# First-stage bursts one step earlier and spread relayout loads in a Fourier mixing and MLP kernel

## The chip, the cores and the metric

The kernel runs on one core of a Trainium2 chip. The metric is the device time of one execution in microseconds. A core has five engines that run on their own and wait for each other through semaphores: TensorE (PE, matmuls; PEld is its weight load), VectorE (DVE), ScalarE (ACT), GpSimd (POOL) and SyncE (SP). In this kernel POOL and SP mostly issue DMA transfers, each from its own queue in order.

## The reference, cut to what matters

```python
X = np.fft.rfft(x, axis=1)                       # x: 8 batches x 3008 rows x 256 channels
Y = X * (filt_r + 1j * filt_i)[None]             # 1505 frequencies x 256 channels
y = np.fft.irfft(Y, n=3008, axis=1)
h = y.reshape(24064, 256) @ w_in                 # 256 -> 2048
s = np.sin(alpha * h)
out = (h + s * s / (alpha + 1e-9)) @ w_out       # 2048 -> 256
```

So each batch goes through a long Fourier transform, a product with a filter and the transform back, and then all 24064 rows go through two matrix products with a sine between them.

## The kernel before

**The second half is the backbone.** The rows are cut into 48 chunks, for pairs of batches, of 512 rows (the one in twelve that starts at column 2560 has 384). `hidden(k, jb)` makes one of 16 blocks of the hidden layer of chunk k: two matmuls `ph` (line 602), a cosine on ACT into `cos_all` (L606), and one operation on DVE that makes `v` (L607). `project(k, u)` multiplies eight blocks of `v` with `w_out` into `po` (L622); ACT copies the sums to `o` (L631), and POOL issues their stores (L666).

**The planner.** The main loop goes through steps. One step has two calls of `hidden` for chunk k, then `slot(step)`, then the projections of chunk k−1 that fall to this step (eight matmuls `po` for each), then `slot(step + 0.5)`. Everything of the Fourier transforms is put into a list beforehand, each entry with the step at which it is due (`put`), and `slot` takes out what is due, in order of due time, with at most one entry of PE work per slot unless an entry is more than a step late. The order of instructions on every engine comes from this list alone. A chunk is eight steps, a pair of batches 96, and the plan of batch b is laid out around z = 48 b, the step at which its rows are first needed.

**The stages of a batch b ≥ 2.**

- `load_x` (L160, POOL): part ch of four of the input, two transfers, due 8 steps ahead of its burst. Each also waits for the last `v` that was issued before it (`after(ins, marks["snake"])`).
- `first_tiled` (L222), a *first-stage burst*: eight matmuls `pa` on a quarter of the array each. They fill four PSUM buffers: two of the pool `fps` (two buffers in all, which `forward` and `last` use too, and `inverse_tiled`) and two of the pool `hps` (four buffers, otherwise used by `ph`). ACT evacuates two of them (L185) and DVE two (L187), and SP stores the result to the scratch tensor `d1` in DRAM (L229).
- `load_t2` (L235, POOL), the *relayout loads*: four loads g of 384 KB from `d1`, in another order of the axes.
- `forward` (L243, 12 units): two matmuls `pb`, evacuated by ACT to `xf` (L246); SP swaps the halves into `xs` (L250). `product` (L257) and `cross` (L263, L264) on DVE multiply with the filter. Loads g = 0 to 3 feed units 0 to 2, 3 to 5, 6 to 8 and 9 to 11.
- `inverse_tiled` (L293), an *inverse burst*, three per batch: sixteen matmuls `pc` into two buffers of `fps` and two of `hps`, three evacuations on ACT and one on DVE, and stores to `d2` (L301).
- `load_t4` (L306, SP) and `last` (L316, 16 blocks u): four matmuls `pd` into one buffer of `fps`, evacuated into `y`, two on ACT to one on DVE in turn (L185, L187).

Batch 1 uses smaller forms of the first stage (L206) and of the inverse (L274), and batch 0 is done ahead of the loop. A buffer of a pool is free again when the evacuation of its last user is done; the next matmul into it waits for that on PE, and with it all that stands behind it.

**Due times that matter here.** `firsts(b)` gives the steps of the four bursts of a batch. For b ≥ 4 they are 48 b − 105.5 + 8 ch. `inverses(b)` gives those of the inverse bursts. `bursts` collects them all. `aside` moves a `product` or a `cross` that is due in the 1.1 steps ahead of a burst to just behind it, and `clear` moves a `forward` or a `last` that would fall right at a burst:

```python
    bursts = [at for b in range(TILED, B) for at in (*firsts(b), *inverses(b))]
...
        return next((s + 1 for s in bursts if s - 0.75 < at <= s + 0.25), at)
...
        return next((s + 0.05 for s in bursts if s - 1.1 < at <= s), at)
```

A `product` follows its `forward` by 1.5 steps and a `cross` by 4.5. Block u of `last` is due at z − 6.5 + u for u < 4 and at z − 11 + 2.6 u after that; block 6 thus at z + 4.6, which `slot(z + 5)` takes, and block 9 at z + 12.4. The forward units of batches 1 and 2 are due from step 18 in steps of 1.21 and from step 51 in steps of 2.2. The bursts of batch 3 are due at 49.5, 54.5, 60.5 and 66.5.

Of the kernel before, what the change touches and what calls it, by code (L numbers as in the profile page):

```python
# [71 lines left out]
def kernel(  # L72
# [599 lines left out]
    def put(at, fn, *args, pe=False):  # L672
        pending.append((at, len(pending), pe, fn, args))

    def firsts(b):

        return {2: (37.5, 39.5, 41.5, 43.5), 3: (49.5, 54.5, 60.5, 66.5)}.get(
            b, [48 * b - 105.5 + 8 * ch for ch in range(4)])

    def inverses(b):  # L680

        return (63.5, 73.5, 81.5) if b == 2 else [48 * b - 46.5 + 16 * w for w in range(3)]

    bursts = [at for b in range(TILED, B) for at in (*firsts(b), *inverses(b))]

    def clear(at):

        return next((s + 1 for s in bursts if s - 0.75 < at <= s + 0.25), at)

    def aside(at):  # L690

        return next((s + 0.05 for s in bursts if s - 1.1 < at <= s), at)
# [9 lines left out]
    for b in range(1, B):  # L702
        s = s1 if b == 1 else Spectral(b)
        z = 48 * b
        if b > 1:
            for ch in range(4):
                put(22 + 4 * ch if b == 2 else firsts(b)[ch] - 8, s.load_x, ch)
        if b < TILED:
            for i in range(16):
                put(6.9 + 0.35 * i, s.first, i, pe=True)  # L710
        else:
            for ch in range(4):
                put(firsts(b)[ch], s.first_tiled, ch, pe=True)
        for g in range(4):
            put(12.5 if b == 1 else 45 if b == 2 else max(70, z - 77 + 12 * g), s.load_t2, g)
        for u in range(12):
            inv = 24 + 1.21 * u if b == 1 else 57 + 2.2 * u if b == 2 else z - 59 + 4 * u
            fwd = inv - 6
            fwd = clear(fwd)
            put(fwd, s.forward, u, pe=True)  # L720
            put(aside(fwd + (0.5 if b == 1 else 1.5)), s.product, u)
            if s.fused:
                put(aside(fwd + (4 if b == 1 else 4.5)), s.cross, u)
            if b < TILED:
                put(inv, s.inverse, u, pe=True)
        if b >= TILED:
            for w in range(3):
                put(inverses(b)[w], s.inverse_tiled, w, pe=True)
        for ch in range(4):
            put(z - (9.5 if b == 1 and ch < 3 else (10.5, 10.5, 10.5, 3)[ch]), s.load_t4, ch)  # L730
        for u in range(16):
            put(clear(z + (u - (5 if b == 1 else 6.5) if u < 4 else 2 * u - 9 if b == 1 else 2.6 * u - 11)),
                s.last, u, pe=True)
# [59 lines left out]
```

## Time and profile before

| | |
|---|---|
| Median of 3 runs | 776.32 us (775.06 to 776.39) |
| The profiled execution's own time | 775.76 us |
| Its span, first to last instruction | 774.0 us |
| Busy: PE, DVE, ACT, POOL | 763.1, 656.5, 611.4, 371.1 us |
| Granted TensorE clock | 1.0 of full speed, all through |
| `ph` L602, `po` L622 on PE | 389.1 us (1536 matmuls), 389.3 us (3008) |
| `v` L607 on DVE, `cos_all` L606 on ACT | 482.8 us, 414.0 us (768 each) |
| Burst matmuls `pa` L222 | 192, from 111.8 to 528.3 us |
| Relayout loads L235 | 28, 384 KB each, median 5.1 us from issue to landing |

How to read it. Busy time of PE is the time in which a matmul is under way, with ends that are modelled, so back-to-back matmuls overlap in the record; starts of matmuls tell more than ends. A line of the timeline gives the start and the length of a run of like instructions on one engine, in microseconds, then engine, line, operation, output and input, and their number; in brackets stands the idle time of the engine before it and who ended it. The list of waits gives engine, line and releaser, then the total in microseconds, the number of waits and the longest.

### The profile page before, as it was taken

The numbers are of one execution on the slowest core, as the hardware profiler recorded it, in microseconds if no ns is written. First come the engines' busy times: TensorE is split into PE (matmuls) and PEld (weight loads), VectorE is DVE, ScalarE is ACT, GpSimd is POOL, SyncE is SP. The second block draws the span as 40 slices with busy tenths as digits, with TensorE's granted clock in tenths as the row PEclk, the third lists the DMA queues.
The fourth block names the chain that finished last, engine by engine and source line by source line (L and its number), as shares of the span: only waits on it lengthen the run. The fifth ranks groups of instructions, "written<-read, shape, count | busy, mean of one in ns | idle before, by whom it ended". The sixth has DMA issues, their size and how long they took to land.

```text
span 774.0 us, 17223 instructions
## 1 busy us (share of the span) xinstructions
PE 763.1 (99%) x6036; PEld 516.6 (67%) x6036; DVE 656.5 (85%) x1172; ACT 611.4 (79%) x1206; POOL 371.1 (48%) x649
## 2 busy tenths in 40 slices
PE   8999999999999999999999999999999999999997
PEld 4757766666666667666666666766666666766666
DVE  6886998999989888898889988899888888777774
ACT  6798988898888877888878787888778777777763
POOL 6455446544645555555565647554554645330000
PEclk9999999999999999999999999999999999999999
DMA  9955678854855438544474536764254322511112
GB/s 221 285 107 168 139 157 262 206 136 111 218 140 138 118 71 221 139 115 124 113 201 109 141 92 151 199 148 120 72 145 106 92 69 55 138 47 32 40 37 60
DMA packets 81518, 101.49 MB, mean 131 GB/s; under 512 B 18884, under 2 KB 60864, under 8 KB 81431
## 3 DMA queue, kind: packets, MB, share of 16 engines
q1 hardware_dynamic: 53503, 52.84, 25.7%
q0 software_dynamic: 27440, 47.29, 25.6%
q8 instruction: 47, 0.77, 0.4%
q14 instruction: 40, 0.33, 0.1%
q10 hardware_dynamic: 488, 0.27, 0.1%
HBM read 56.15 MB, written 46.66 MB: 133 GB/s over the span
## 4 chain that ended last, share of the span: by engine, by line
PE 90%; DMA 4%; DVE 3%; ACT 1%; issue 0%; POOL 0%; SPq 0%; POOLq 0%
PE po L622 41%; PE ph L602 40%; DVE v L607 3%; PE pd L316 2%; PE pb L243 2%; PE pa L222 2%; DMA d_t<-d_tbl 1%; PE pc L293 1%; DMA w_out<-in_moe_w_out_dram 1%; DMA filt_t<-in_filt_r_dram 1%; DMA w_in<-in_moe_w_in_dram 1%; ACT cos_all L606 1%; PE pa L206 0%; PE pc L274 0%; POOL x L168 0%
## 5 line engine op out<-in xcount | busy, mean ns | idle before, releaser
L607 DVE SCALAR_TENSOR_TENSOR v<-cos_all,ph 128x512 f16<-128x512 f32 (+1 forms) x768 | 482.8, 672 | 95.6 <-ACT cos_all L606 92.3
L606 ACT ACTIVATE cos_all<-ph 128x512 f32<-128x512 f32 (+1 forms) x768 | 414.0, 600 | 99.5 <-PE ph L602 98.2
L666 POOL DMA_DIRECT2D out_dram<-o x530 | 291.7, 557 | 242.4 <-ACT o L631 214.9
L602 PE MATMUL ph<-y,w 128*128 128x512 f16 (+1 forms) x1536 | 389.1, 375 | 1.3 <-DVE v L607 1.1
L622 PE MATMUL po<-w,v 128*128 128x256 f16 x3008 | 389.3, 273 | 0.0
L622 PEld LDWEIGHTS <-v 128*128 128x128 f16 x3008 | 290.1, 98 | 84.2 <-issue 1.1
L602 PEld LDWEIGHTS <-w 128*128 128x128 f16 x1536 | 143.2, 98 | 113.9 <-issue 19.0
L631 ACT COPY o<-po 128x512 f32<-128x512 f32 (+1 forms) x95 | 56.1, 590 | 7.8 <-PE po L622 7.2
L246 ACT CAST xf<-pb 128x512 f16<-128x512 f32 x84 | 51.1, 608 | 1.3 <-PE pb L243 0.8
L185 ACT CAST y<-pd 128x376 f16<-128x376 f32 (+1 forms) x86 | 42.1, 491 | 12.3 <-PE pd L316 8.8
L160 POOL DMA_DIRECT2D x<-in_x_dram x48 | 25.6, 538 | 41.7 <-DVE v L607 26.9
L185 ACT CAST t_h<-pa 128x512 f16<-128x512 f32 (+1 forms) x60 | 32.8, 590 | 12.5 <-PE pa L222 11.3
L316 PEld LDWEIGHTS <-t_a 96*128 96x128 f16 x448 | 31.4, 97 | 12.7
L264 DVE TENSOR_TENSOR p<-p,xs 128x512 f16<-128x512 f16 x84 | 35.7, 425 | 2.9
L263 DVE TENSOR_TENSOR xs<-xs,filt_t 128x512 f16<-128x512 f16 x84 | 35.2, 419 | 2.0 <-DMA xs<-xf 2.0
L257 DVE TENSOR_TENSOR p<-xf,filt_t 128x512 f16<-128x512 f16 x84 | 35.1, 419 | 0.0
L185 ACT CAST gt<-pc 128x512 f16<-128x512 f32 x54 | 28.2, 595 | 8.4 <-PE pc L293 8.4
L187 DVE CAST t_h<-pa 128x512 f16<-128x512 f32 (+1 forms) x52 | 33.5, 683 | 0.2
L243 PE MATMUL pb<-t,d_t 128*128 128x256 f16 x168 | 32.1, 273 | 0.0
L316 PE MATMUL pd<-wh_t,t_a 96*128 96x94 f16 x384 | 31.8, 204 | 0.0
L235 POOL DMA_DIRECT2D t<-d x28 | 24.4, 874 | 11.3 <-DMA d<-t_h 9.4
L243 PEld LDWEIGHTS <-d_t 128*128 128x128 f16 x168 | 16.3, 98 | 14.3
(70 smaller groups left out, 276.4 us busy)
## 6 DMA issues: line engine op xcount, KB each, us to landing
t<-d POOLq DMA_DIRECT2D x28, 384.0 KB, 5.1
xs<-xf SPq DMA_DIRECT2D x168, 64.0 KB
t_a<-d SPq DMA_DIRECT2D x28, 384.0 KB
x<-in_x_dram POOLq DMA_DIRECT2D x50, 188.0 KB, 4.5
d<-t_h SPq DMA_DIRECT2D x48, 192.0 KB
d<-gt SPq DMA_DIRECT2D x36, 256.0 KB
out_dram<-o POOLq DMA_DIRECT2D x91, 64.0 KB, 2.1
out_dram<-o POOLq DMA_DIRECT2D x31, 80.0 KB, 3.5
```

Source lines behind the costliest of these rows:

```text
L185: marks["act"] = nc.scalar.copy(out=dst, in_=src)
L243: nc.tensor.matmul(out=ps[:, i, :], lhsT=d_t[:, s, :], rhs=self.t2[s // 6][:, s % 6, :], start=True, stop=True)
L246: nc.scalar.copy(out=self.xf[u], in_=ps)
L263: nc.vector.tensor_tensor(out=xs, in0=xs, in1=f_t[1][:, 2 * u:2 * u + 2, :], op=ALU.mult)
L264: nc.vector.tensor_tensor(out=p, in0=p, in1=xs, op=ALU.add)
L316: nc.tensor.matmul(out=psv[:, i, :], rhs=wi_t if self.b < TILED else wh_t, start=True, stop=True, lhsT=t4_h[ch // 2][0:NK, n0 % 16 + i, cb ...
L602: nc.tensor.matmul(out=ps[:, 0:n], lhsT=w1[:, cb, jb * 128:jb * 128 + 128], rhs=y_cols[:, cb, c0:c0 + n], start=(cb == 0), stop=(cb == 1))
L606: nc.scalar.activation(out=cs[:, 0:n], in_=ps[:, 0:n], func=AFT.Sin, bias=float(np.pi / 2))
L607: marks["snake"] = nc.vector.scalar_tensor_tensor(out=v[k][:, jb, 0:n], in0=cs[:, 0:n], scalar=-1.0, in1=ps[:, 0:n], op0=ALU.add, op1=ALU. ...
L622: nc.tensor.matmul(out=pso[k][:, t % 2, :], lhsT=v[k][:, jb, 128 * t:128 * t + 128], rhs=w2[:, jb, :], start=(jb == 0), stop=(jb == 15))
L631: copy(out=o[:, i0:t % 2 + 1, :], in_=pso[k][:, i0:t % 2 + 1, :])
L666: queues[i % len(queues)].dma_start(out=bass.AP(tensor=out.tensor, offset=out.offset + t0 * C, ap=[*ap, [1, C]]), in_=o_blk[p0:p0 + rows, :])
```

## The change

All four first-stage bursts of each batch from 4 on come one step sooner, which moves their `load_x` one step sooner with them, and `bursts` as well. The second load of batch 3 (ch = 1) is due at step 45 instead of 46.5. The four relayout loads of batch 1 are due at steps 13.5, 14, 17 and 20 instead of all at 12.5, and those of batch 2 at 46.5, 49, 53 and 59 instead of all at 45.

```diff
     def firsts(b):
         return {2: (37.5, 39.5, 41.5, 43.5), 3: (49.5, 54.5, 60.5, 66.5)}.get(
-            b, [48 * b - 105.5 + 8 * ch for ch in range(4)])
+            b, [48 * b - 106.5 + 8 * ch for ch in range(4)])
...
             for ch in range(4):
-                put(22 + 4 * ch if b == 2 else firsts(b)[ch] - 8, s.load_x, ch)
+                put(22 + 4 * ch if b == 2 else 45 if (b, ch) == (3, 1) else firsts(b)[ch] - 8, s.load_x, ch)
...
         for g in range(4):
-            put(12.5 if b == 1 else 45 if b == 2 else max(70, z - 77 + 12 * g), s.load_t2, g)
+            put((13.5, 14, 17, 20)[g] if b == 1 else (46.5, 49, 53, 59)[g] if b == 2 else max(70, z - 77 + 12 * g), s.load_t2, g)
```

## The prediction, made before the result was known

> **What bounds the kernel now.** I read the page first, parts 1 and 4 (busy time, and the chain that ended last):
>
> ```profile
> PE 763.1 (99%) x6036; PEld 516.6 (67%) x6036; DVE 656.5 (85%) x1172; ACT 611.4 (79%) x1206; POOL 371.1 (48%) x649
> ...
> PE 90%; DMA 4%; DVE 3%; ACT 1%; issue 0%; POOL 0%; SPq 0%; POOLq 0%
> ```
>
> PE is busy for 99% of the span and carries 90% of the chain. Ends of matmuls are modelled, so I next asked for PE's own waits between 66 and 764 us, the stretch in which everything that the change touches lies:
>
> ```profile
> PE ph L602 <- DVE v L607: 0.6, 3, 0.2
> PE pd L403 <- ACT xf L246: 0.4, 1, 0.4
> ```
>
> The reader sees total, times and longest: 1.0 us in 698. Busy time can hide waits under the modelled ends, so I went through the starts of PE's matmuls in the timeline. Two hidden blocks and 8 projections, one step of the planner, take 1.74 us. A first-stage burst adds 0.65 us, all 24 the same to within 3 ns, so none of the 16 that move waits now. Three inverse bursts (L293) do wait: 0.41 us near 181 us, 0.53 us near 319 and 0.53 us near 503. PE is the bound, and only what makes it wait, or stop waiting, counts.
>
> **The bursts (16, each one step sooner).** The built programs have the same 6036 matmuls, 1172 DVE and 1206 ACT operations; SP's order is the same. Each burst (8 matmuls) passes 4 matmuls `ph` and 8 `po`; its two ACT and two DVE evacuations pass two `cos_all` and two `v`; and one product L257 (0.42 us on DVE) goes from two steps ahead of the burst to just behind it, since `aside` now catches it. So PE's work stays the same: 0 us. What decides is whether the PSUM buffers are free one step sooner. The pair of the four-buffer pool waits for the same distance in `v` as now: 0. The pair of the two-buffer pool `fps` takes the buffers of the two last users. For parts 0, 1 and 3 of a batch the last user lies at least a whole step back. For part 2 it doesn't: block 6 of the last stage (planned at z+4.6, run at step z+5) stood 1.5 steps ahead of the burst, and now stands half a step ahead. Batch 6, timeline:
>
> ```profile
> 419.41 1.04 PE L622 MATMUL po<-w,v 128*128 128x256 f16 x8
> ...
> 420.29 1.03 PE L602 MATMUL ph<-y,w 128*128 128x512 f16 x4
> ...
> 421.00 0.55 DVE L187 CAST y<-pd 128x376 f16<-128x376 f32 x1
> ...
> 422.12 0.63 PE L222 MATMUL pa<-x,wt_t 47*64 47x512 f16 x8
> ```
>
> Columns: start, length, what; block 6's matmuls `pd` stand just ahead, at 419.24. The burst will stand where `ph` starts at 420.29. A burst starts 0.09 us later than a `ph` there (last `po` of eight starts at 421.92; a `ph` would follow 0.11 later, the burst starts at 422.12), so at 420.38. The `y` evacuation, queued on DVE behind two `v`, ends at 421.55 only, or about 421.4 with the product gone from ahead of it. Here the built program puts both `fps` tiles of the burst in one bank, the second waiting for ACT's cast of the first. The cast starts 0.45 us behind a burst (row below: 314.00, 314.45), takes 0.59, and PE starts 0.05 after (a `v` ends at 320.06, `ph` starts at 320.11): 0.45 + 0.59 + 0.05 = **1.09 us**.
>
> In batches 4, 5 and 7 the second tile waits for ACT's `y`. Batch 5:
>
> ```profile
> 326.69 0.51 ACT L185 CAST y<-pd 128x376 f16<-128x376 f32 x1
> ...
> 326.91 0.59 PE L602 MATMUL ph<-y,w 128*128 128x512 f16 x2
> ```
>
> The burst would start at 326.91 + 0.09 = 327.00; its second tile may start at 327.20 + 0.05 = 327.25: 0.25 us. Batch 7, likewise: `ph` at 510.71, `y` 510.50 to 511.00: 0.25 us. Batch 4: `ph` at 236.48, `y` ends at 236.66: 0.14 us. Behind such a wait PE's whole queue stands; nothing later waits now, so nothing gives it back. Sum: 1.09 + 0.25 + 0.25 + 0.14 = +1.73 us.
>
> The waits near 319 and 503 come five to six us behind a moved burst. The first of them:
>
> ```profile
> 314.00 0.63 PE L222 MATMUL pa<-x,wt_t 47*64 47x512 f16 x8
> 314.45 1.07 ACT L185 CAST t_h<-pa 128x512 f16<-128x512 f32 x2 [0.67 <-PE pa L222]
> ...
> 316.62 0.65 ACT L631 COPY o<-po 128x512 f32<-128x512 f32 x1
> ...
> 317.46 2.15 ACT L606 ACTIVATE cos_all<-ph 128x512 f32<-128x512 f32 x4
> ...
> 320.11 1.19 PE L602 MATMUL ph<-y,w 128*128 128x512 f16 x4 [0.19 <-DVE v L607]
> ```
>
> ACT has no gap from 316.16 to 319.62: copies and casts push `cos_all` to 317.46, hence `v` to 318.18, hence PE. With the burst's casts one step sooner, ACT is free earlier, but its copy at 316.62 needs the last `po`, which ends at 316.47: it can start at 316.52, 0.10 us sooner. So 0.10 of 0.53 us goes, twice: −0.2 us; bounds 0 and −1.06. What is late next is that copy.
>
> The Trainium skill speaks against the move: "TensorEngine Tiling (Array Packing)", Performance Considerations, holds that tiling speeds up TensorE but not the PSUM evacuation, which may become the limit. By that rule alone every moved burst would wait for a cast as batch 6's does, 16 x 1.09 = 17 us. The trace agrees only in part: three of the inverse bursts wait, none of the first-stage bursts does, so by the rows the four cases above stay the sum.
>
> **The relayout loads.** Batch 1: loads 0 and 1 keep their place on POOL; 2 and 3 go behind 7 and 14 output stores. They have the room: they land at 73.6 and 74.9 us now and their first forward matmuls come at 87.3 and 94.7. Moved by about 4 and 10 us, both still land ahead. Cost 0. Batch 2 on POOL:
>
> ```profile
> 130.16 3.34 POOL L235 DMA_DIRECT2D t<-d  x4 [3.62 <-DMA d<-t_h]
> 133.49 1.10 POOL L160 DMA_DIRECT2D x<-in_x_dram  x2
> ```
>
> Load 0 waits for batch 2's `d` stores, lands at 133.97, and the forward matmul needs it at 137.26: 3.3 us of room. The change puts the two loads of `x` part (3,1) ahead of it, into POOL's idle time; they share the DMA engines with the last `d` store. Bounds: nothing, and 2.0 us (two such loads land 1.0 us apart) plus a landing of 5.0 us instead of 3.8: 3.2 us, within the room. I take 0. Loads 1 to 3 then stand behind stores that take 0.53 us each, with 13, 25 and 37 us of room. `x` (3,1) lands 1.5 us ahead of its burst now and some 10 after; that gain is 0 in this execution. The `x` loads of batches 4 and later keep their order on POOL and land 5.4 us or more ahead; a step costs 1.74 of that.
>
> **Sum.** +1.73 − 0.2 + 0 = +1.5 us. The profiled execution took 775.76 us (span 774.0), so 777.3; it lies 0.56 under the median of the runs, 776.32, so the median should be **777.8**.
>
> **Rivals.**
> 1. *No wait at part 2*: three of four waits are under 0.3 us, and if `y` comes out first and the one-bank case costs little, what is left is −0.2: 776.1. Against it: the bank order stands in the built program.
> 2. *Slower: load 0 of batch 2 becomes the wait.* If the `d` store and then the load each lose more than the room of 3.3 us together, PE stops at the first forward matmul of batch 2, priced 1 us for 4.3 us lost: 778.8. It decides from a landing at 137.26. For it: the DMA engines are 100% busy from 124 to 127 us. Against: they are all but idle from 130.1 to 131.6, and can catch up there.
>    The Trainium skill gives such a delay a cause, "SBUF — State Buffer", SBUF: two separate sides: while DVE holds the shared port, GpSimd can't write descriptors, and a transfer of 620 ns took 3100. By it, an estimate of 2.5 us on load 0, still within its room; the 28 issues of L235 take 825 to 904 ns each, so this trace shows no such lock.
> 3. *Faster*: both inverse waits vanish (−1.06), part 2 is free, and in usual executions `x` (3,1) comes late today (the median lies 0.56 above the profile): 776.32 − 1.06 − 0.56 = 774.7.
>
> **Chances.** A measurement can tell about 0.2% from no change: 1.55 us, 774.77 to 777.87. Forecast, 777.8, sits just under the edge: 0.62, split by the gain near 319 and 503, 0.37 within and 0.25 above. Rival 1: 0.16, within. Rival 2: 0.16, above. Rival 3: 0.06, below. So faster 0.06, same 0.53, slower 0.41. Range 775.6 to 779.0: the low end is rival 1 less the 0.56 us by which usual executions exceed the profile, should a late `x` (3,1) be what they lose; the high end is rival 2 with no gain near 319 and 503.
>
> **What would show it.** In the profile after: PE starting `pa` twice, 1.1 us apart, near 420 us, and shorter breaks near 237, 327 and 511; the break near 319 and 503 still some 0.4 us; load 0 of batch 2 landing ahead of its `pb`. Wrong if PE shows no break within a part 2 burst, or one at the first `pb` of batch 2.

## The result, and the profile after

The changed kernel took 776.87 us (median of 15 runs, 776.32 to 778.23), the kernel before 775.29 (median of 15 runs taken beside them, 774.85 to 776.79). The ratio is 1.0017, with a 95% interval of 1.001 to 1.0024: **1.6 us slower**, where +1.5 was forecast. The median of before is 1.0 us lower than that of the three runs from which the prediction started, so the time itself, 777.8, was forecast 0.9 too high; the difference was not.

The page after, parts 1 and 4:

```profile
PE 763.4 (99%) x6036; PEld 516.9 (67%) x6036; DVE 656.6 (85%) x1172; ACT 612.7 (79%) x1206; POOL 370.9 (48%) x649
...
PE 90%; DVE 4%; ACT 3%; DMA 2%; issue 1%; POOL 1%; POOLq 0%
```

PE has the same work and is as busy as before. ACT has 3% of the chain instead of 1%, but that isn't the loss: most of it lies in the first 66 us, ahead of everything that the change moves, where the chain passes through ACT for 13.3 us in this profile and for 2.0 in the one before. The list of PE's waits from 66 to 764 us names the place:

```profile
PE pa L222 <- ACT t_h L185: 0.7, 1, 0.7
PE pd L403 <- ACT xf L246: 0.4, 1, 0.4
PE ph L602 <- DVE v L607: 0.2, 1, 0.2
```

The first line wasn't there before: a burst matmul waits for ACT's cast of the same burst. It is the burst of batch 6, part 2, in the timeline:

```profile
419.21 0.33 PE L316 MATMUL pd<-wh_t,t_a 96*128 96x94 f16 x4
...
420.35 0.40 PE L222 MATMUL pa<-x,wt_t 47*64 47x512 f16 x2
420.80 0.58 ACT L185 CAST t_h<-pa 128x512 f16<-128x512 f32 x1 [0.73 <-PE pa L222]
420.81 0.54 DVE L187 CAST y<-pd 128x376 f16<-128x376 f32 x1
421.43 0.62 PE L222 MATMUL pa<-x,wt_t 47*64 47x512 f16 x6 [0.68 <-ACT t_h L185]
```

The eight `pa` are broken in two: two matmuls at 420.35, six at 421.43. Between them ACT's cast runs from 420.80 to 421.38. PE shows 0.68 us idle, but from start to start the break is 1.08 us: the first part ends, as modelled, only at 420.75. The other three breaks of part 2 don't show as idle time at all; I read them from the starts of the `pa`, where an undisturbed burst takes 761 ns from the start of the matmul ahead of it (a `po`) to the start of the one behind it (a `ph`):

| burst, part 2 of batch | at us | takes ns | break us | predicted |
|---|---|---|---|---|
| 4 | 236.22 | 886 | 0.13 | 0.14 |
| 5 | 326.61 | 1005 | 0.24 | 0.25 |
| 6 | 420.35 | 1836 | 1.08 | 1.09 |
| 7 | 511.68 | 1003 | 0.24 | 0.25 |

In batches 4, 5 and 7 the third `pa`, the first one into the second buffer of `fps`, starts 0.05 us behind the end of ACT's `y` of block 6. Batch 5:

```profile
326.30 0.51 ACT L185 CAST y<-pd 128x376 f16<-128x376 f32 x1
326.61 0.87 PE L222 MATMUL pa<-x,wt_t 47*64 47x512 f16 x8
```

That `y` ends at 326.80, the third `pa` starts at 326.85. Behind the burst of batch 5 there is one more break, not foreseen: the third `ph`, at 328.00, starts 0.15 us late. The inverse bursts near 319 and 503 us still wait, 0.36 us each instead of 0.53. Here is the first:

```profile
316.29 0.58 ACT L631 COPY o<-po 128x512 f32<-128x512 f32 x1
...
317.13 2.09 ACT L606 ACTIVATE cos_all<-ph 128x512 f32<-128x512 f32 x4
...
317.78 2.48 DVE L607 SCALAR_TENSOR_TENSOR v<-cos_all,ph 128x512 f16<-128x512 f32 x4 [0.51 <-ACT cos_all L606]
...
318.95 0.63 PE L293 MATMUL pc<-p,e_t 64*64 64x256 f16 x16
```

Measure each from the inverse burst: the copy starts 2.66 us ahead of it (2.56 before: 319.18 − 316.62), the first `v` 1.17 (1.00 before). The relayout loads of batch 2 and `x` (3,1), in the timeline of POOL:

```profile
127.19 1.05 POOL L160 DMA_DIRECT2D x<-in_x_dram  x2 [0.99 <-PE ph L602]
130.28 0.88 POOL L235 DMA_DIRECT2D t<-d  x1 [2.03 <-DMA d<-t_h]
```

Load 0 lands at 134.61, 2.3 us ahead of its `pb`; `x` (3,1) lands at 133.16, 8.8 us ahead of its burst.

For all that follows one number stands for each kernel, *the stretch*: the time from the start of the 289th `ph` matmul to that of the 1249th, about 177 to 637 us. It holds every burst of batches 4 to 7. PE's order outside the moved work is the same in it, so it repeats to within 0.02 us where the programs are alike. Before: 459.31 us. After: 460.78, so +1.47. The breaks above give 1.69 + 0.15 − 0.17 − 0.17 = +1.50. That accounts for the result.

### The profile page after: what moved, and what is told of

It reads as the page before. It is cut to its first block, busy times and chain, and to the rows that moved or that the text cites. A ratio compares the mean times of both kernels' runs of the same rounds, so it can differ in the third digit from the quotient of the medians.

```text
span 774.8 us, 17223 instructions
## 1 busy us (share of the span) xinstructions
PE 763.4 (99%) x6036; PEld 516.9 (67%) x6036; DVE 656.6 (85%) x1172; ACT 612.7 (79%) x1206; POOL 370.9 (48%) x649
## 4 chain that ended last, share of the span: by engine, by line
PE 90%; DVE 4%; ACT 3%; DMA 2%; issue 1%; POOL 1%; POOLq 0%
PE po L622 41%; PE ph L602 40%; DVE v L607 3%; PE pd L316 2%; PE pb L243 2%; PE pa L222 2%; DMA w<-id 1%; PE pc L293 1%; ACT t_h L185 1%; ACT cos_all L606 1%; PE pa L206 0%; ACT xf L494 0%; PE pd L403 0%; PE warm L437 0%; DMA x<-in_x_dram 0%
## 5 line engine op out<-in xcount | busy, mean ns | idle before, releaser
L264 DVE TENSOR_TENSOR p<-p,xs 128x512 f16<-128x512 f16 x84 | 35.7, 425 | 2.9
L263 DVE TENSOR_TENSOR xs<-xs,filt_t 128x512 f16<-128x512 f16 x84 | 35.0, 416 | 0.5 <-DMA xs<-xf 0.5
L257 DVE TENSOR_TENSOR p<-xf,filt_t 128x512 f16<-128x512 f16 x84 | 34.9, 417 | 0.0
L235 POOL DMA_DIRECT2D t<-d x28 | 24.7, 884 | 9.7 <-DMA d<-t_h 8.3
```

The costliest lines, as they stand in the source:

```text
L263: nc.vector.tensor_tensor(out=xs, in0=xs, in1=f_t[1][:, 2 * u:2 * u + 2, :], op=ALU.mult)
L264: nc.vector.tensor_tensor(out=p, in0=p, in1=xs, op=ALU.add)
```

## The experiments

My theory: PE waits in part 2 for the buffers of `fps`, because block 6 of `last` now stands half a step ahead of the burst; all else is worth little. The rivals were that the relayout loads cost the time, or that every moved burst costs a share. Each ratio is to the kernel before, run beside it, with its 95% interval.

**1. The bursts alone, and the loads alone.**

The kernel `bursts_only` is the changed one with

```diff
-                put(22 + 4 * ch if b == 2 else 45 if (b, ch) == (3, 1) else firsts(b)[ch] - 8, s.load_x, ch)
+                put(22 + 4 * ch if b == 2 else firsts(b)[ch] - 8, s.load_x, ch)
...
-            put((13.5, 14, 17, 20)[g] if b == 1 else (46.5, 49, 53, 59)[g] if b == 2 else max(70, z - 77 + 12 * g), s.load_t2, g)
+            put(12.5 if b == 1 else 45 if b == 2 else max(70, z - 77 + 12 * g), s.load_t2, g)
```

and `loads_only`, the same kernel as `loads_again`, is the changed one with

```diff
-            b, [48 * b - 106.5 + 8 * ch for ch in range(4)])
+            b, [48 * b - 105.5 + 8 * ch for ch in range(4)])
```

> The bursts of batches 4 and later one step sooner, loads as before. Theory (the short waits of PE within the part 2 bursts are the whole cost): the same breaks as after, +0.12, +0.24, +1.08 and +0.24 us in the part 2 bursts near 236, 327, 420 and 512 us, +0.15 at the ph behind the one near 327, -0.17 each at the inverse bursts near 319 and 503; in all some 1.5 us above before, as after. Rival (the loads cost the time): within 0.3 us of before.

> The loads moved as in the change, the bursts where they were. Theory: PE's breaks as in before, load 0 of batch 2 landing some 2 us ahead of its first pb; within 0.3 us of before. Rival (the loads cost the time): some 1.5 us above before, with a new break of PE between 60 and 150 us.

> The same kernel as in the run with the loads alone, measured once more, since that one came out at a ratio of 0.9991 with an interval that ends at 0.9999. Theory (the loads are worth nothing, PE's path between 177 and 637 us is that of before): within 0.3 us of before, the interval around 1. Rival (x part (3,1), which landed only 0.8 to 1.5 us ahead of its burst in three profiles with the old loads, lands late in some executions, and the change mends this): again 0.3 to 0.5 us below before.

The bursts alone: 776.96 us, ratio 1.0019 [1.001, 1.0029], stretch 460.78, as after, with the same breaks at the same bursts. The loads alone: 775.12, ratio 0.9991 [0.9982, 0.9999], stretch 459.30, as before. That interval just misses 1; the same kernel run again gave 775.74, 0.9997 [0.9983, 1.0011], stretch 459.30. The loads are worth nothing that can be told. `x` (3,1) landed 8.2 us ahead of its burst with them and 0.8 without (the kernel with the bursts alone): room that nothing used in any profile.

**2. Part 2 put back, and part 2 alone.**

The kernel `part2_back` is the changed one with

```diff
-            b, [48 * b - 106.5 + 8 * ch for ch in range(4)])
+            b, [48 * b - 106.5 + 8 * ch + (ch == 2) for ch in range(4)])
```

and `part2_alone` is the kernel before with

```diff
-            b, [48 * b - 105.5 + 8 * ch for ch in range(4)])
+            b, [48 * b - 105.5 + 8 * ch - (ch == 2) for ch in range(4)])
```

> The changed kernel with only the part 2 bursts of batches 4 to 7 back at their old step. Theory: the four breaks of part 2 and the one behind the burst near 327 us are gone, the gains near 319 and 503 us stay (they belong to other parts): 0.3 us below before and 1.8 below after. Rival (moving any burst costs, or the loads do): three quarters of the 1.5 us stay, 1.2 us above before, with breaks elsewhere.

> The kernel before with only the part 2 bursts of batches 4 to 7 one step sooner. Theory: the breaks of part 2 alone, 0.12 + 0.24 + 1.08 + 0.24 us, with 0.15 behind the second of them: 1.7 to 1.85 us above before, and the waits near 319 and 503 us unchanged at 0.53 each. Rival (each moved burst costs alike): a quarter of 1.5 us, 0.4 above before.

Part 2 alone: 777.3 us, ratio 1.0019 [1.0011, 1.0028], stretch 460.98, +1.67. Its four bursts take 886, 1004, 1836 and 1003 ns, and the inverse waits stay at 0.53. A quarter of the moved bursts thus holds all of the loss. But the 0.15 us expected behind the burst of batch 5 did not come. DVE's order is the same there as after the change; what differs is the wait near 319, still 0.53. Where that wait is 0.17 shorter, PE reaches the burst sooner and DVE doesn't: its first `v` behind the last `cross` starts 1.13 us ahead of the burst after the change, 1.30 with part 2 alone. So the 0.15 is the gain near 319 given back eight us later.

Part 2 put back: 775.72, 1.0 [0.9991, 1.0009], stretch 459.30. The four breaks are gone, as the theory had it. The 0.3 us below before did not come: the gains near 319 and 503 are there (0.17 each), but new breaks of 0.2 us behind part 2 of batch 5 (near 329) and 0.16 behind part 3 of batch 6 (near 437), now seven steps behind part 2, take them back.

**3. Which engine empties block 6.** Of the four blocks 6 that stand ahead of a part 2 burst, the one ahead of batch 6's (it is a block of batch 4, which is two batches behind) is the only one whose `y` DVE evacuates; it comes late, behind `v`. If that is why both tiles of the burst got one bank, the engine decides between 0.13 and 1.08 us.

The kernel `block6_on_act` is the changed one with the edit below, `block6_on_dve` has False in place of True.

```diff
-            evac(y[:, cb, self.b % 2, n0:n0 + 4, :], psv)
+            evac(y[:, cb, self.b % 2, n0:n0 + 4, :], psv, True if u == 6 and self.b > 1 else None)
```

> The changed kernel with y of block 6 evacuated by ACT in every batch from 2 on; in batch 6 it was DVE's. Theory (what PE waits for is the evacuation that holds the second buffer of the pool fps; in batch 6 both tiles fell into one bank because DVE's y comes late): the break of 1.08 us near 420 us falls to 0.1 to 0.25, the other three stay; 0.8 to 0.95 us less than after from 177 to 637 us, 0.6 above before. Rival (the break of batch 6 has another cause, its step or the loads): stays at 1.08.

> The changed kernel with y of block 6 evacuated by DVE in every batch from 2 on. Theory: all four part 2 bursts get both tiles of fps in one bank and break for 1.08 us each, 4.3 us in all instead of 1.69; 2.6 us above after, 4.1 above before. Rival (the break of batch 6 has another cause): the breaks stay at 0.12, 0.24, 1.08 and 0.24, within 0.3 us of after.

With ACT the burst of batch 6 is one piece in the timeline:

```profile
420.02 0.48 ACT L185 CAST y<-pd 128x376 f16<-128x376 f32 x1
420.42 0.75 PE L222 MATMUL pa<-x,wt_t 47*64 47x512 f16 x8
```

Its `y` ends at 420.50, 0.08 us into the burst, and the burst takes 886 ns instead of 1836, a break of 0.13 us. The stretch is 459.84, 0.94 less than after. The time, 776.24 us, is that of a single run.

With DVE all four break. The list of PE's waits:

```profile
PE pa L222 <- ACT t_h L185: 3.0, 4, 0.8
```

and the burst of batch 4, which waited 0.13 us in after:

```profile
235.95 0.40 PE L222 MATMUL pa<-x,wt_t 47*64 47x512 f16 x2
236.40 0.59 ACT L185 CAST t_h<-pa 128x512 f16<-128x512 f32 x1 [0.73 <-PE pa L222]
236.42 0.54 DVE L187 CAST y<-pd 128x376 f16<-128x376 f32 x1
237.04 0.62 PE L222 MATMUL pa<-x,wt_t 47*64 47x512 f16 x6 [0.68 <-ACT t_h L185]
```

The bursts take 1836, 1986, 1836 and 1986 ns: 4.60 us of breaks, where 4.3 was expected. In batches 5 and 7 ACT's copy `o` stands ahead of the cast, which starts 0.59 us behind the burst there instead of 0.45. 459.31 + 4.60 − 0.34 (the two gains) = 463.57; the stretch took 463.56. In time 779.89 us, ratio 1.0052 [1.0038, 1.0066], or 4.3 us. The cost follows the one evacuation, up and down.

**4. Block 6 out of the way, the bursts where the change has them.**

The kernel `block6_later` is the changed one with the edit below, `block6_earlier` has 3.5 in place of 6.

```diff
-            put(clear(z + (u - (5 if b == 1 else 6.5) if u < 4 else 2 * u - 9 if b == 1 else 2.6 * u - 11)),
+            put(clear(z + (u - (5 if b == 1 else 6.5) if u < 4 else 2 * u - 9 if b == 1 else 6 if b > 1 and u == 6 else 2.6 * u - 11)),
```

> The changed kernel with block 6 of the last stage due at step z + 6, behind the part 2 burst instead of half a step ahead of it. Theory: no break in any part 2 burst, and the gains near 319 and 503 us stay; 1.5 to 1.85 us less than after, 0 to 0.35 below before, unless block 7, now close behind block 6, or the ph behind the burst waits in turn. Rival (the burst's own evacuations at that step are what is late, not block 6): the breaks stay, as after.

> The changed kernel with block 6 of the last stage due at step z + 3.5, one step sooner, so that it stands 1.5 steps ahead of the part 2 burst as in before. Theory: no break in any part 2 burst, and the gains near 319 and 503 us stay; 1.5 to 1.85 us less than after, 0 to 0.35 below before. Rival (the burst's own evacuations at that step are what is late, not block 6): the breaks stay, as after.

Later: 775.5 us, 0.9998 [0.9989, 1.0007], stretch 459.66. Earlier: 775.47, 0.9996 [0.9987, 1.0005], stretch 459.45. Either takes most of the loss away, 1.12 and 1.33 of 1.47 us, so it was block 6 and not the burst's own step. But neither beats before, and the expectation failed in part. With block 6 later the burst of batch 5 still breaks and takes 1179 ns: its seventh `pa` and then the `ph` behind it wait for DVE's `v`. With block 6 earlier its eight `pa` stand together, but the first and the third `ph` behind it wait, 0.25 and then 0.17 us:

```profile
324.20 0.42 DVE L263 TENSOR_TENSOR xs<-xs,filt_t 128x512 f16<-128x512 f16 x1
324.66 0.42 DVE L264 TENSOR_TENSOR p<-p,xs 128x512 f16<-128x512 f16 x1
325.00 2.47 DVE L607 SCALAR_TENSOR_TENSOR v<-cos_all,ph 128x512 f16<-128x512 f32 x4
...
326.12 0.63 PE L222 MATMUL pa<-x,wt_t 47*64 47x512 f16 x8
...
326.93 1.19 PE L602 MATMUL ph<-y,w 128*128 128x512 f16 x4 [0.18 <-DVE v L607]
```

The two operations of a `cross`, 0.42 us each, stand ahead of the four `v` on DVE, and `ph` waits for the third and the fourth of these. That gave a new theory: the `v` are late because a `cross` now stands ahead of them.

**5. Products and crosses behind the burst.** With 2.1 steps in place of 1.1, `aside` catches the `cross` too.

The kernel `products_only` is the kernel before with this edit, `products_behind` is `block6_earlier` with it:

```diff
-        return next((s + 0.05 for s in bursts if s - 1.1 < at <= s), at)
+        return next((s + 0.05 for s in bursts if s - 2.1 < at <= s), at)
```

The kernel `products_first` is `block6_earlier` with

```diff
-        return next((s + 0.05 for s in bursts if s - 1.1 < at <= s), at)
+        late = [s for b in range(4, B) for s in firsts(b)]
+        return next((s + 0.05 for s in bursts if s - (2.1 if s in late else 1.1) < at <= s), at)
```

In the first two kernels the wider window also holds for inverse bursts: the last `cross` that an inverse burst reads comes behind it, so this burst takes a product that isn't finished. The third leaves these in place.

> The kernel before with the products and crosses of the last 2.1 steps ahead of a burst (instead of 1.1) moved behind it. Theory: the 0.53 us each near 319 and 503 are ACT's lateness, not DVE's, so at most 0.1 of each goes; the same as before within 0.3 us. Rival (they are DVE's v late behind the cross): up to 1.06 us below before.

> The changed kernel with block 6 due at z + 3.5 and the products and crosses of the last 2.1 steps ahead of a burst (instead of 1.1) moved behind it, so that DVE's v ahead of the burst is not held up by two of 0.42 us. Theory (what is left behind the part 2 burst near 327 us, 0.4 us, and part of the 0.36 near 319 and 503 is DVE's v being late behind the cross): the 0.4 us near 327 goes, and 0 to 0.7 us near 319 and 503; from 177 to 637 us 458.3 to 459.1 us, 0.2 to 1.0 less than before. Rival (the work only comes later): the products make the v behind the bursts late in turn, and PE waits there as much or more; 459.3 or above.

> The changed kernel with block 6 due at z + 3.5, and with the products and crosses of the last 2.1 steps ahead of a first-stage burst of batches 4 and later (of the others, 1.1 as now) moved behind it. Theory (the 0.25 + 0.15 us left behind the part 2 burst near 327 us are DVE's v, late behind the cross that now stands ahead of the burst; the 0.36 each near 319 and 503 are ACT's copies and casts): the 0.4 us near 327 goes, 0.36 near 319 and 503 and 0.42 near 181 stay; from 177 to 637 us 459.0 us, 0.3 less than before; in time 0.3 us below before and 1.8 below after. Rival (the work only comes later): breaks of as much behind other bursts; 459.3 or above.

Products only: 777.04 us, 1.0022 [1.0012, 1.0032], stretch 460.35. It tells who holds the inverse burst near 319 us:

```profile
317.50 2.15 ACT L606 ACTIVATE cos_all<-ph 128x512 f32<-128x512 f32 x4
...
318.20 2.48 DVE L607 SCALAR_TENSOR_TENSOR v<-cos_all,ph 128x512 f16<-128x512 f32 x4 [0.88 <-ACT cos_all L606]
...
319.20 0.75 PE L293 MATMUL pc<-p,e_t 64*64 64x256 f16 x16
```

DVE is now idle for 0.88 us ahead of `v`, waiting for ACT, and the burst breaks as before (1141 ns): ACT's lateness, as the prediction had it, and not DVE's. My expectation of "the same as before" was wrong all the same: PE breaks newly near 167, 187 to 190, 325, 359 and 424 us.

Products behind: 776.31, 1.0015 [1.0006, 1.0024], stretch 459.75. The 0.4 us near 327 is gone, and 0.42 near 181 with it, and the 0.36 near 319 and 503 stays. But more is lost elsewhere: 0.6 us from 187 to 190, 0.29 near 324, 0.15 near 359 and 0.12 near 325.

Products first: 776.74, 1.0016 [1.0007, 1.0025], stretch 460.29. The 0.4 us near 327 shrinks to 0.10, so in this kernel the place of the `cross` made most of it. The price is larger: new breaks of 0.37 us behind the inverse bursts near 412 and 444, and 0.2 more at those near 319 and 503. Ahead of the one near 412:

```profile
409.90 0.42 DVE L263 TENSOR_TENSOR xs<-xs,filt_t 128x512 f16<-128x512 f16 x1
...
410.36 0.42 DVE L264 TENSOR_TENSOR p<-p,xs 128x512 f16<-128x512 f16 x1
...
410.70 2.47 DVE L607 SCALAR_TENSOR_TENSOR v<-cos_all,ph 128x512 f16<-128x512 f32 x4
...
411.86 0.63 PE L293 MATMUL pc<-p,e_t 64*64 64x256 f16 x16
```

The first `v` of the four starts 1.16 us ahead of the burst here. With block 6 earlier and the products in place it starts at 409.75, 1.96 ahead of the burst at 411.71, and nothing waits. DVE, now with the `cross` behind the first-stage burst, has no idle time above 0.04 us from 407.1 to 413 us, so its delay was passed on to the next burst. The rival held, for products behind too; none of these three kernels is faster than before.

## Why the prediction was right, point by point

- **PE is the bound, the rest is idle anyway.** Held. All of the loss is in PE's breaks (+1.50 by breaks, +1.47 by the stretch).
- **The three parts that have their last `fps` user a step away cost nothing.** Held: the bursts of parts 0, 1 and 3 take 761 ns each after the change, and part 2 alone gives +1.67.
- **Part 2: 1.09 + 0.25 + 0.25 + 0.14.** Held: 1.08, 0.24, 0.24 and 0.13. That block 6 is the cause was argued from the built order; experiments 3 and 4 show it. That the second tile waits for the burst's own cast where DVE empties block 6, and for `y` where ACT does, is shown by 3 as well; that the two tiles share a bank then is read from the program, no trace shows banks.
- **"Nothing later waits now, so nothing gives it back".** Held for the breaks themselves, not for what follows: 0.15 us was lost at a `ph` behind part 2 of batch 5. The prediction followed the product (L257), but not the `cross` (L263, L264): four `v` behind it stand ahead of the burst's evacuations now, and six did before, so DVE has less of a lead. And it took the waits as separate terms. Part 2 alone has the same `cross` at the same place and no such wait; what PE gained near 319 is what DVE could not follow near 327.
- **The waits near 319 and 503: 0.10 each.** The direction and the cause (ACT's copy) held, the size was 0.17. The copy came 0.10 sooner as worked out; the other 0.07 lie between `cos_all` and `v`, 0.65 us apart instead of 0.72, and why is not shown. With the 0.15 the errors cancel, by luck: the sum was +1.53 and the breaks +1.50.
- **The relayout loads: 0.** Held, by two runs of them alone. Rival 2 needed load 0 of batch 2 to lose all of its 3.3 us of room; 2.3 us were left after the change, 1.9 and 1.5 in the two runs of the loads alone, and 1.25 at the least in the other profiles, so its condition came nearer but never held. The smallest room is that of load 0 of batch 1, which the change leaves in its place: PE waited for it 0.05 us near 70.3 after the change and 0.07 with part 2 alone, which has the loads of before. The Trainium skill's rule in "SBUF — State Buffer", SBUF: two separate sides, by which DVE can hold up the writing of descriptors, isn't seen here either: the 28 issues of L235 take 847 to 912 ns after the change.
- **The rule of the Trainium skill that evacuation may limit tiled matmuls** ("TensorEngine Tiling (Array Packing)", Performance Considerations), taken for every burst, gave 17 us. The trace agrees for one of the 16, batch 6's, which waits 1.08 us for its own cast; the other three of part 2 wait 0.13 to 0.24 us for the evacuation of block 6, and 12 don't wait.
- **The time.** The forecast of 777.8 rests on a median of three runs, two of which lay near 776.35; fifteen gave 775.29. The measured 776.87 is the forecast difference on a lower base.

What stays open: what sets the spread of single runs of before, 774.8 to 776.8 us in the fifteen, which is larger than the effect. In the profiles the first `ph` starts anywhere from 35.8 to 36.6 us; I made no experiment on it.

## What to carry to other kernels

When a block of work moves in a hand-made order, list for each buffer pool it takes from who used it last at the old and at the new place, and which engine empties that user: here one evacuation, on one engine or the other, made 0.13 or 1.08 us. Moving that user by a step took away 1.1 or 1.3 of the 1.5 us here. But with DVE 85% busy a delay that was pushed off one burst arrived at the next, and 0.17 us that PE gained at one wait was lost again at another, so count the breaks over the whole stretch and not at the place that was mended. Read breaks from the starts of matmuls: the list of waits showed 0.7 of 1.08 us and none of the three smaller ones.

## What I had not expected of the hardware

The same eight matmuls break by 0.13 or by 1.08 us, by which evacuation they wait for. The idle time of PE in the record is 0.40 us shorter than the break (0.68 against 1.08), because the modelled end of the matmul ahead lies that much behind its start. And the stretch of 459 us, with 960 `ph` in it, repeats to 0.01 us between profiles of the same PE order (459.31, 459.30, 459.30), while whole runs of one kernel spread by 2 us: differences of 0.1 us can be read from the breaks that no timing of this kernel can tell.
